# Entry 0's opening in a Fourier-mixing and SoLU kernel: x as stationary operand of the first transform step, its result kept on chip, and the loads and adds around it in another order

## The chip, the cores and the metric

The kernel runs on one core of a Trainium2 chip. The metric is the device time of one execution in microseconds, as the median of several runs. A profile of one execution gives the start and duration of the instructions on each engine: TensorE (PE for matmuls, PEld for loads of the stationary operand), VectorE (DVE), ScalarE (ACT), GpSimd (POOL) and SyncE (SP, which only issues DMAs). ACT and POOL issue DMAs as well.

## The reference

Eight entries of 3136 tokens by 256 channels go through a global filter (a real Fourier transform along the tokens, a product with a complex filter, the inverse transform). All 25,088 tokens then go through a feed-forward block: a product with `w_in`, the SoLU (h times its softmax) with layer normalization, and a product with `w_out`.

```python
def _attn_ref(x, filt_r, filt_i):                 # x: 8 x 3136 x 256
    X = np.fft.rfft(x, axis=1)
    Y = X * (filt_r + 1j * filt_i)[None, :, :]    # 1569 x 256
    return np.fft.irfft(Y, n=x.shape[1], axis=1).astype(np.float32)

def _moe_ref(x, w_in, w_out, g_ln):               # 256 -> 1024 -> 256
    h = x @ w_in
    e = np.exp(h - np.max(h, axis=-1, keepdims=True))
    solu = h * (e / (np.sum(e, axis=-1, keepdims=True) + 1e-09))
    mu = np.mean(solu, axis=-1, keepdims=True)
    var = np.mean((solu - mu) ** 2, axis=-1, keepdims=True)
    return (((solu - mu) / np.sqrt(var + 1e-06) * g_ln) @ w_out).astype(np.float32)
```

`x` and the filters are 4-byte floats; `w_in`, `w_out` and `g_ln` arrive as 8-byte floats.

## The kernel before

**Tiling of the transform.** The 3136 tokens of an entry are seen as 49 (n1) by 64 (n2). A first step transforms over n1 and leaves 25 residues s (`NS`), each with 128 rows (real and imaginary parts of the sums and differences of mirrored n2) and 256 channels. A second step transforms over those rows, residue by residue, with tables `de`. Seven units follow one another, each of four residues but for the last, which has one. A unit is `forward` (matmuls `pb`), `multiply` by the filter (two products on DVE and one add for each of two parts), `inverse` (matmuls `pc`), two ACT copies to `g`, and a store to the DRAM scratch `d2`. The last step (`back`, matmuls `py`) reads `d2` in the other order (the tile `t4`) and fills `y`, the tokens of the feed-forward block.

**The opening** (lines 402 to 604) does this for entry 0 alone, before the main loop, in the order written out by hand. Each engine executes its own instructions, and each queue issues its DMAs, in that order:

1. Lines 512 to 524: loads of x of entry 0 (SP for one half of n2, POOL for the mirrored half, in eight pieces), of the first two pieces of weights (`begin`) and of `de` and filters for the first eight pairs of residues.
2. Lines 525 to 530: the first step, piece by piece. The stationary operand is the 98 x 100 table `wf`, x is the moving one (512 columns), an ACT copy evacuates, and the result goes to the DRAM scratch `d1`.
3. Line 541: `idle_row`, matmuls whose result nobody reads. Lines 547 and 548: `convert` of two pieces of weights from 8 to 4 bytes. Each takes a row of DVE operations, one ACT multiplication (L442) and two POOL operations (L443, L447) for the `w_in` pieces; for the `w_out` pieces L445 on DVE stands in place of L442 and L443.
4. Lines 557 to 564: unit 0's rows are scattered within the chip by 16 DMAs (SP and ACT in turn), and the rows of units 1 to 6 are read back from `d1` by SP, with nine loads of tables for the last residues among them.
5. Lines 565 to 582: the units. `start(i + 2)` comes before unit i's `multiply`, so PE runs ahead by two units. The add of the first part is on DVE, that of the second on POOL; an `idle` matmul stands before each `inverse`. POOL issues four small loads after unit 0 and one `begin` in later units.
6. Lines 583 to 604: 14 `idler` matmuls; SP reads `d2` back in eight pieces, each as 96 rows and 4 rows (L181, L182); `fetch_second` loads six pieces of x of entry 1 (L462); four stores put the filters into `f_dram`; the other weights are converted, `weight_sums` is formed on DVE, and PE runs `back`, 128 rows of the profile in all.

Only units 0 to 5 write what the 96-row reads need; the 4-row reads need unit 6.

**The main loop** (`step`, from line 948) has 196 + 9 steps. A step issues products with `w_in` (L723), the SoLU, products with `w_out` (L844), and jobs of the transforms of entries 1 to 7 at steps fixed by `PLAN`. Its first products need `y` of entry 0 and `w_in`; its first transform jobs need the pieces from `fetch_second`.

One form of matmul of the loop matters for the text: `back_halves` (L372) multiplies 50 x 64 stationary blocks with 49 moving columns in the four quarters of the array, 32 matmuls a call. The profile counts each matmul of this kernel as two records.

Of the kernel before, what the change touches and what calls it, by code (L numbers as in the profile page):

```python
# [49 lines left out]
def dft_tables():  # L50
# [39 lines left out]
    return wf.reshape(NR, NK).astype(f32), wq.reshape(P, 2, 64).astype(f32), \  # L90
# [4 lines left out]
def kernel(  # L95
# [11 lines left out]
    wf_host, wq_host, wi_host, wb_host, de_host = dft_tables()  # L107
# [76 lines left out]
    class Spectrum:  # L184
# [5 lines left out]
        def __init__(self, e, pools, load, load_de):  # L190
            self.e, self.pools = e, pools
            self.load, self.load_de = load, load_de
            self.spare = {}
            self.units = [(i, min(2, NP - i)) for i in range(0, NP, 2)]
            self.xs, self.t1s, self.t2s, self.fs, self.prods, self.gs, self.des, self.spectra, self.diffs = (
                {} for _ in range(9))
# [115 lines left out]

        def multiply(self, i, part, add=nc.vector.tensor_tensor):
# [15 lines left out]
        def inverse(self, i, pss):  # L329
            de, prods = self.des.pop(i), self.prods.pop(i)  # L330
            for r in range(2):
                for u in range(self.shape(i)[0]):
                    rows = slice(NQ * u, NQ * u + NQ)
                    self.product(i, pss[u][NQ * r:NQ * r + NQ], lambda v: de[rows, v, 1, r, :],
                                 prods[r][rows])
# [11 lines left out]
    def fetch_first_back(ch):  # L347
        by_16((nc.sync.dma_start, nc.sync.dma_start), t4s[0, ch],
              d2[0].rearrange("s (a n) c -> (s a) n c", a=4)[:, NCH * ch:NCH * ch + NCH, :])
# [52 lines left out]
    with ExitStack() as st:  # L402
        fpool = pool("fp", 1, stack=st)
        pools = {name: pool(name + "0", bufs, stack=st)
                 for name, bufs in (("r", 1), ("t2", 1), ("p", 2), ("g", 2))}
# [3 lines left out]
        def load_words(src, n):  # L409
            raw = wpool.tile([P, 512, 2], I32, name=f"raw_{n}", tag="raw")  # L410
            nc.gpsimd.dma_start(
# [48 lines left out]
        def fetch_second():  # L460
            for i in range(6):
                second.fetch_x(i, [lambda out, in_: nc.sync.dma_start(out=out, in_=in_)] * 2,  # L462
                               spare_piece(i))

        def load_tables(i0, n, dma):
            de = fpool.tile([P, n, 2, 2, NQ], FP32, name=f"de_{i0}", tag=f"de{i0}")
            dma(out=de, in_=de_dram[i0:i0 + n].rearrange("i p k u q -> p i (k u q)"))
            f = fpool.tile([P, n, 2, C], FP32, name=f"f_{i0}", tag=f"f{i0}")
# [26 lines left out]
        def begin(j):  # L495
            raws[j] = load_words(weights[j][1], j)

# [4 lines left out]
        rows_x = pools["r"].tile([P, NH, C], FP32, name="x_0", tag="r")  # L502

        def fetch_x(h, n0, n, r0, rows, dma):

            first, step = (n0, C) if h == 0 else (N2 - 1 - n0, -C)
            dma(out=rows_x[N1 * h + r0:N1 * h + r0 + rows, n0:n0 + n],
                in_=bass.AP(tensor=x.tensor, offset=x[0].offset + r0 * N2 * C + first * C,
                            ap=[[N2 * C, rows], [step, n], [1, C]]))

        st.enter_context(tc.manual_schedule())
        nc.sync.dma_start(out=wf_t, in_=wf_dram)
        pieces = NH // NCH

        fetch_x(0, 0, NCH, 0, N1 - 1, nc.sync.dma_start)
        fetch_x(0, 0, NH, N1 - 1, 1, nc.sync.dma_start)
        for i in range(pieces):
            if i:
                fetch_x(0, NCH * i, NCH, 0, N1 - 1, nc.sync.dma_start)
            fetch_x(1, NCH * i, NCH, 0, N1, nc.gpsimd.dma_start)  # L520
            if i in (4, 7):
                begin(i // 7)
        load_tables(0, 4, nc.gpsimd.dma_start)
        load_tables(4, 4, nc.gpsimd.dma_start)
        for i in range(pieces):
            sp.xs[i] = rows_x[:, NCH * i:NCH * i + NCH]

            sp.first(i, (0, 1), ps_h.tile([P, 2, 512], FP32, name=f"pa_0_{i}", tag="h"),
                     nc.scalar.copy, sp.xs[i][0:NK])
            sp.store_first(i, 0, lambda out, in_: by_16((nc.scalar.dma_start, nc.sync.dma_start), out, in_))  # L530
# [10 lines left out]
        idle_row(8, "idle")  # L541
# [5 lines left out]
        for j in range(2):  # L547
            convert(j)

        def start(i):  # L550
            sp.fetch_filter(i)
            sp.fetch_de(i)
            sp.forward(i, halves(f"pb_0_{i}"))
# [3 lines left out]
        sp.t2s[0] = t2_0 = pools["t2"].tile([P, 4, C], FP32, name="t2_0_0", tag="t2")  # L557
        for n in range(16):
            (nc.sync, nc.scalar)[n % 2].dma_start(
                out=t2_0[NH * (n % 4):NH * (n % 4) + NH, n // 4, :], in_=rows_x[n:n + 1])  # L560
        for i in range(1, units):
            sp.fetch(i, nc.sync.dma_start, spare_piece(i - 1))
            if i == 2:
                load_tables(8, NP - 8, nc.sync.dma_start)
        for i in range(2):
            start(i)
        for i in range(units):
            if i + 2 < units:
                start(i + 2)
            sp.multiply(i, 0, nc.vector.tensor_tensor)  # L570
            sp.multiply(i, 1, nc.gpsimd.tensor_tensor)
            pss = [ps_t.tile([P, 2, C], FP32, name=f"pc_0_{i}_{u}", tag="t") for u in range(2)]
            idle(pss[0])
# [7 lines left out]
            elif i != 2:  # L581
                begin({1: 2, 3: 3, 4: 4, 5: 5, 6: 6}[i])
# [4 lines left out]
        for ch in range(pieces):  # L587
            fetch_first_back(ch)
        fetch_second()
# [5 lines left out]
        convert(2)  # L595
        begin(7)
        convert(3)
        convert(4)
        weight_sums(w_in_sb)
        for j in (5, 6, 7):  # L600
# [490 lines left out]
```

## Time and profile before

| | |
|---|---|
| median of 3 runs | 1635.9 us (1630.59 to 1640.13) |
| the profiled execution | 1630.59 us, its span 1628.8 us |
| granted TensorE clock of that execution, mean | 0.986 |
| busy over the span | PE 1551.8 us, DVE 1299.9, POOL 1170.6, ACT 903.6 |
| first matmul of the opening | at 8.94 us |
| unit 0's first matmul | at 45.58 us |
| unit 6's store issued | at 81.03 us |
| first product of the main loop | at 106.06 us |

The page gives each engine's busy time, and then the span in 40 slices of 40.7 us. The opening fills the first two and a half. Times of single instructions come from the timeline (start, duration, engine, line, operation, operands, count, and in brackets the idle time before and what ended it). The table of windows gives, for a stretch, each engine's busy time with its number of records, the mean granted clock (PEclk, 1.00 is full), the busy share of the DMA engines, and GB/s.

### The profile page before, as it was taken

What the parts mean: (1) busy time and instruction counts of PE and PEld (TensorE: products, weight loads), DVE (VectorE), ACT (ScalarE), POOL (GpSimd) and SP (SyncE); (2) the same over time, 40 slices, a digit from 0 to 9 for tenths busy, and PEclk for the clock granted to TensorE, in tenths of its full rate; (3) what the DMA queues carried; (4) which work ended last, traced back from release to release, by engine and by line L of the source; (5) the groups of instructions that cost most, each with busy time, mean ns of one, the idle gap of its engine ahead of it and who ended that gap; (6) DMA issues with size and microseconds to landing.
All of it is one profiled execution on the core that took longest, in us unless ns stands there. A gap on an engine that the chain in (4) does not pass through costs nothing. (4 is left out here: it accounts for less than half of the span.)

```text
span 1628.8 us, 36999 instructions
## 1 busy us (share of the span) xinstructions
PE 1551.8 (95%) x12710; PEld 1048.4 (64%) x12710; DVE 1299.9 (80%) x2630; ACT 903.6 (55%) x1772; POOL 1170.6 (72%) x1333
## 2 busy tenths in 40 slices
PE   5798789999999999999999999999999999999997
PEld 1353356666765676666666676666676777777776
DVE  1686777898897989987899779888888777777772
ACT  2134455566565556566556656566555665565662
POOL 4445887678776877797578866888576766677775
PEclk8999999999999999999999999999999999999999
DMA  9888868877788778875787668866875554444443
GB/s 265 245 268 250 231 187 231 230 204 198 206 239 219 198 194 230 240 202 149 222 232 226 186 177 225 239 175 165 222 227 152 130 131 127 104 111 103 110 110 101
DMA packets 377245, 312.13 MB, mean 192 GB/s; under 512 B 62762, under 2 KB 342835, under 8 KB 377059
## 3 DMA queue, kind: packets, MB, share of 16 engines
q1 hardware_dynamic: 304340, 168.63, 40.4%
q0 software_dynamic: 34624, 101.68, 20.8%
q10 hardware_dynamic: 38096, 39.46, 8.0%
q8 instruction: 103, 1.69, 0.5%
q14 instruction: 82, 0.67, 0.1%
HBM read 124.86 MB, written 81.50 MB: 127 GB/s over the span
## 5 line engine op out<-in xcount | busy, mean ns | idle before, releaser
L844 PEld LDWEIGHTS o<-w_out_sb,solu_t 128*128 128x128 f32 x3136 | 383.2, 193 | 51.2 <-issue 43.6
L844 PE MATMUL o<-w_out_sb,solu_t 128*128 128x128 f32 x3136 | 402.2, 276 | 4.1 <-DVE ot L860 3.3
L723 PE MATMUL m<-w_in_sb,s 128*128 128x512 f32 x784 | 397.9, 609 | 8.4 <-ACT h L733 4.7
L844 PEld LDWEIGHTS o<-w_out_sb,u 128*128 128x128 f32 x2352 | 308.0, 192 | 144.4 <-issue 106.2
L844 PE MATMUL o<-w_out_sb,u 128*128 128x128 f32 x2352 | 311.8, 276 | 7.4 <-ACT ot L856 4.7
L723 PE MATMUL m<-w_in_sb,y 128*128 128x512 f32 x588 | 310.0, 610 | 9.2 <-DVE nmax L747 7.1
L771 DVE SCALAR_TENSOR_TENSOR h<-e,rsum,h 128x1024 f32<-128x1024 f32 x196 | 302.7, 1544 | 6.9
L733 ACT COPY h<-m 128x512 f32<-128x512 f32 x294 | 173.2, 589 | 236.7 <-PE m L723 203.4
L702 POOL TENSOR_TENSOR u<-solu_t 128x512 f32<-128x512 f32 x98 | 139.2, 1420 | 227.4 <-DMA solu_t<-turn 133.4
L856 ACT ACTIVATE ot<-o,rs_t 128x128 f32<-128x128 f32 x392 | 143.8, 367 | 259.5 <-PE o L844 241.5
L779 ACT ACTIVATE h<-h,nmu 128x1024 f32<-128x1024 f32 x196 | 225.0, 1148 | 53.4 <-DVE turn L787 53.0
L747 DVE CUSTOM_DVE_ANT_0 h<-m,h 128x512 f32<-128x512 f32 x196 | 133.8, 682 | 145.2 <-ACT h L733 102.0
L787 DVE STREAM_TRANSPOSE turn<-h 128x1024 f32<-128x1024 f32 x196 | 243.1, 1240 | 3.3
L755 ACT ACTIVATE e<-h,nmax 128x1024 f32<-128x1024 f32 x196 | 225.1, 1148 | 10.4 <-DVE h L771 9.9
L702 POOL TENSOR_TENSOR u<-solu_t,u 128x512 f32<-128x512 f32 x98 | 152.6, 1557 | 91.5 <-PE o L844 87.5
L723 PEld LDWEIGHTS m<-w_in_sb,s 128*128 128x128 f32 x784 | 129.2, 192 | 97.2 <-issue 84.6
L723 PEld LDWEIGHTS m<-w_in_sb,y 128*128 128x128 f32 x588 | 95.8, 191 | 108.7 <-issue 49.0
L702 POOL TENSOR_TENSOR u<-u,solu_t 128x512 f32<-128x512 f32 x98 | 164.1, 1674 | 0.9
L860 DVE SCALAR_TENSOR_TENSOR ot<-o,rs_t,ot 128x128 f32<-128x128 f32 x294 | 101.9, 346 | 75.8 <-ACT ot L856 58.4
L702 POOL TENSOR_TENSOR solu_t<-solu_t,solu_t 128x512 f32<-128x512 f32 x98 | 147.5, 1506 | 7.7
L702 POOL TENSOR_TENSOR s<-y 128x128 f32<-128x128 f32 x196 | 97.0, 495 | 0.4
L372 PEld LDWEIGHTS py<-wb_t,t 50*64 50x64 f32 x3584 | 57.8, 134 | 44.3 <-issue 20.9
(116 smaller groups left out, 1961.7 us busy)
## 6 DMA issues: line engine op xcount, KB each, us to landing
solu_t<-turn SPq DMA_DIRECT2D x784, 128.0 KB
out_dram<-ot SPq DMA_DIRECT2D x196, 128.0 KB
t<-d POOLq DMA_DIRECT2D x112, 200.0 KB, 6.2
d<-x POOLq DMA_DIRECT2D x100, 200.0 KB, 5.3
f<-f_dram POOLq DMA_DIRECT2D x39, 512.0 KB, 7.0
d<-g POOLq DMA_DIRECT2D x39, 512.0 KB, 4.9
t<-d ACTq DMA_DIRECT2D x37, 512.0 KB
x<-in_x_dram SPq DMA_DIRECT2D x112, 98.0 KB
```

The lines of the kernel that those rows point to most:

```text
L372: nc.tensor.matmul(out=views[g][64 * h:64 * h + 64, cb, i, :], lhsT=t4[rows, i, c0:c0 + 64], rhs=wb_t[rows, 0:N1], start=True, stop=True)
L702: nc.gpsimd.tensor_tensor(out=out, in0=in0, in1=in1, op=op)
L723: nc.tensor.matmul(out=ms[j, bank], lhsT=lhsT, rhs=w_in_sb[:, w, :], start=m in (1, 2, 7), stop=True, skip_group_check=True)
L733: nc.scalar.copy(out=h_half(k, i), in_=ms[j, 0])
L747: nc.vector.tensor_tensor_reduce(out=h_half(k, i), in0=ms[j, bank], in1=h_half(*kept), scale=1.0, scalar=sofar, op0=ALU.add, op1=ALU.min, ...
L755: nc.scalar.activation(out=e, in_=hs[k], func=AFT.Exp, bias=nmaxs.pop(k)[:, 1:2], scale=-1.0, accum_out=esum)
L771: nc.vector.scalar_tensor_tensor(out=solu, in0=e, scalar=rsum, in1=solu, op0=ALU.mult, op1=ALU.mult, accum_out=nmu)
L779: nc.scalar.activation(out=solu, in_=solu, func=AFT.Square, bias=nmu, scale=-float(DFF), accum_out=variances[g][:, i:i + 1])
L787: nc.vector.transpose(out=turns[g][:, :, i, :], in_=solus[k].rearrange("p (f j) -> p f j", j=32))
L844: nc.tensor.matmul(out=pos[p, bank], lhsT=lhs[:, f, :], rhs=w[:, f, :], start=f == 0 and m in (1, 2, 7), stop=True, skip_group_check=True)
L856: nc.scalar.activation(out=out_half(p, *to)[0], in_=pos[p, 0], func=AFT.Copy, scale=rs)
L860: nc.vector.scalar_tensor_tensor(out=ot, in0=pos[p, bank], scalar=rs, in1=out_half(p, *kept)[0], op0=ALU.mult, op1=ALU.add)
```

## The change

**x by channel.** x of entry 0 lies on chip in two blocks of 64 partitions (128 channels each, n1 on the partitions), so a DMA run is 512 bytes in place of 1 KB. SP loads one block and ACT the other, in four quarters of n2. Before them DVE and POOL clear partitions 32 to 63, in four pieces. DVE (POOL for two of eight) forms sums and differences of mirrored n2 in `y`, which is still free.

**First step with x as stationary operand.** For each of 128 channels there are four matmuls: a 49 x 64 block of x is stationary, and 25 columns of a small table `wx` move. Seven groups of up to 20 channels are evacuated by one ACT copy each, straight into the rows that the second step reads. `d1` of entry 0, its stores and read-backs, the scatter and the `idle` row are gone. Eight `warm` matmuls go before the groups, one `keep` matmul follows each.

**Units.** `forward_whole` multiplies with all 128 rows at once and 64 stationary columns, in place of 64 x 64 blocks. It has its own tables `de0`, half as large again. Both adds are on POOL. The `idle` before `inverse` is gone.

**Order.** All tables and filters go through SP behind x. Weights 0 to 3 are begun by POOL ahead of the units; three `convert`s stand before the units and the fourth behind them. Behind the units SP reads all eight 96-row pieces of `d2` first and the eight 4-row pieces after them, then loads weights 4 and 5, three pieces of entry 1, weights 6 and 7, and three more pieces; the stores of the filters follow.

```diff
+        def forward_whole(self, i, pss):
+            de, i0 = self.des[i], self.units[i][0]
+            for v in range(self.units[i][1]):
+                for r in range(2):
+                    for u in range(self.shape(i)[0]):
+                        nc.tensor.matmul(out=pss[r][NQ * u:NQ * u + NQ, v, :], lhsT=de[:, v, r, u, :],
+                                         rhs=self.turned[:, 2 * (i0 + v) + u, :], start=True, stop=True)
+            self.spectra[i] = pss
...
-    def fetch_first_back(ch):
-        by_16((nc.sync.dma_start, nc.sync.dma_start), t4s[0, ch],
-              d2[0].rearrange("s (a n) c -> (s a) n c", a=4)[:, NCH * ch:NCH * ch + NCH, :])
+    def fetch_first_back(ch, part):
+        rows = (slice(0, 96), slice(96, NK))[part]
+        nc.sync.dma_start(out=t4s[0, ch][rows], in_=d2[0].rearrange("s (a n) c -> (s a) n c", a=4)[
+            rows, NCH * ch:NCH * ch + NCH, :])
...
+        nc.sync.dma_start(out=wx_t, in_=wx_dram)
+        pieces = NH // NCH
+        quarter = NH // 4
+        for i in range(4):
+            (nc.vector, nc.gpsimd)[i % 2].memset(x_q[32:64, :, quarter * i:quarter * i + quarter, :], 0.0)
+        for i in range(4):
+            for h in range(2):
+                fetch_x(0, h, quarter * i, quarter, 0, N1 - 1, nc.sync.dma_start)
+                fetch_x(1, h, quarter * i, quarter, 0, N1 - 1, nc.scalar.dma_start)
+            if i == 0:
+                for h in range(2):
+                    fetch_x(0, h, 0, NH, N1 - 1, 1, nc.sync.dma_start)
+                    fetch_x(1, h, 0, NH, N1 - 1, 1, nc.scalar.dma_start)
         nc.sync.dma_start(out=wf_t, in_=wf_dram)
-        for i in range(pieces):
-            sp.xs[i] = rows_x[:, NCH * i:NCH * i + NCH]
-
-            sp.first(i, (0, 1), ps_h.tile([P, 2, 512], FP32, name=f"pa_0_{i}", tag="h"),
-                     nc.scalar.copy, sp.xs[i][0:NK])
-            sp.store_first(i, 0, lambda out, in_: by_16((nc.scalar.dma_start, nc.sync.dma_start), out, in_))
...
+        for i0, n in ((0, 4), (4, 4), (8, NP - 8)):
+            load_tables(i0, n, nc.sync.dma_start)
...
+        for i in range(4):
+            mirror(i, 0, nc.vector)
+            mirror(i, 1, nc.gpsimd if i % 2 else nc.vector)
+            if i == 1:
+                begin(0)
+            if i == 3:
+                for n in range(8):
+                    nc.tensor.matmul(out=ps_t.tile([P, 512], FP32, name=f"warm_{n}", tag="t"),
+                                     lhsT=sums_x[both, :, 0, 16], rhs=sums_x[both, 0:64, 0, 16:24],
+                                     start=True, stop=True)
+                for j in (1, 2, 3):
+                    begin(j)
+
+        for c0 in range(0, P, 20):
+            n = min(20, P - c0)
+            ps = ps_h.tile([P, 2, 512], FP32, name=f"pa_0_{c0}", tag="h")
+            for k in range(n):
+                for g in range(2):
+                    for part in range(2):
+                        rows = slice(64 * g, 64 * g + N1)
+                        nc.tensor.matmul(
+                            out=ps[64 * part:64 * part + 64, g, NS * k:NS * k + NS],
+                            lhsT=sums_x[rows, c0 + k, :, :].rearrange("p j m -> p (j m)"),
+                            rhs=wx_t[rows, part, 0:NS], start=True, stop=True)
+            nc.scalar.copy(
+                out=rows_x[:, 0:NS, :].rearrange("p s (g c) -> p g s c", g=2)[:, :, :, c0:c0 + n],
+                in_=ps[:, :, 0:NS * n].rearrange("p g (k s) -> p g s k", s=NS))
+            nc.tensor.matmul(out=ps_t.tile([P, 512], FP32, name=f"keep_{c0}", tag="t"),
+                             lhsT=sums_x[both, :, 0, 16], rhs=sums_x[both, 0:64, 0, 16:24],
+                             start=True, stop=True)
...
-        idle_row(8, "idle")
...
-        for j in range(2):
+        for j in range(3):
             convert(j)
...
-            sp.forward(i, halves(f"pb_0_{i}"))
+            sp.forward_whole(i, halves(f"pb_0_{i}"))
...
-        sp.t2s[0] = t2_0 = pools["t2"].tile([P, 4, C], FP32, name="t2_0_0", tag="t2")
-        for n in range(16):
-            (nc.sync, nc.scalar)[n % 2].dma_start(
-                out=t2_0[NH * (n % 4):NH * (n % 4) + NH, n // 4, :], in_=rows_x[n:n + 1])
-        for i in range(1, units):
-            sp.fetch(i, nc.sync.dma_start, spare_piece(i - 1))
-            if i == 2:
-                load_tables(8, NP - 8, nc.sync.dma_start)
...
-            sp.multiply(i, 0, nc.vector.tensor_tensor)
+            sp.multiply(i, 0, nc.gpsimd.tensor_tensor)
             sp.multiply(i, 1, nc.gpsimd.tensor_tensor)
...
-            idle(pss[0])
...
-            elif i != 2:
-                begin({1: 2, 3: 3, 4: 4, 5: 5, 6: 6}[i])
+        convert(3)
         idle_row(14, "idler")
...
-        for ch in range(pieces):
-            fetch_first_back(ch)
-        fetch_second()
+        for part in range(2):
+            for ch in range(pieces):
+                fetch_first_back(ch, part)
+        for j in (4, 5):
+            begin(j, nc.sync.dma_start)
+        fetch_second(0, 3)
+        for j in (6, 7):
+            begin(j, nc.sync.dma_start)
+        fetch_second(3, 6)
...
-        convert(2)
-        begin(7)
-        convert(3)
-        convert(4)
         weight_sums(w_in_sb)
-        for j in (5, 6, 7):
+        for j in (4, 5, 6, 7):
             convert(j)
```

## The prediction

> **What bounds the kernel now.** I read the windows first, to see where the time is not the main loop's.
>
> ```profile
> 45.60:81.00 35.40, 26.32 (x218) 12.70 (x218) 25.52 (x42) 6.82 (x13) 14.14 (x16) 0.90 0.91 268
> 81.00:91.50 10.50, 10.50 (x26) 4.57 (x25) 10.19 (x15) 1.34 (x2) 6.13 (x5) 1.00 0.74 243
> 91.50:106.00 14.50, 14.50 (x130) 14.38 (x129) 14.15 (x24) 7.30 (x15) 3.08 (x2) 1.00 0.81 226
> ...
> 200.00:1570.00 1370.00, 1350.12 (x11611) 934.63 (x11604) 1152.60 (x2352) 812.05 (x1608) 1025.16 (x1162) 1.00 0.69 187
> ```
>
> After 200 us PE works 98.5% of the time, and nothing there is changed. The change can only move the point at which the loop begins, at 106 us. The timeline gives the chain up to it.
>
> ```profile
> 28.78 1.22 ACT L442 ACTIVATE raw<-raw 128x512 f32<-128x512 int32 x2 [0.76 <-DMA f<-in_filt_r_dram]
> ...
> 35.49 10.16 PE L534 MATMUL idle<-f,de 128*128 128x512 f32 x16 [8.86 <-DMA f<-in_filt_i_dram]
> ...
> 39.84 1.32 POOL L443 TENSOR_TENSOR raw<-raw,power 128x512 f32<-128x512 f32 x1
> ...
> 45.58 0.68 PEld L301 LDWEIGHTS pb<-t,de 64*64 64x64 f32 x14 [0.76 <-PE idle L534]
> ...
> 52.73 1.27 POOL L324 TENSOR_TENSOR pi<-pi,pt 128x512 f32<-128x512 f32 x1 [7.61 <-DVE pt L323]
> ...
> 78.51 0.37 ACTq L343 DMA_DIRECT2D d<-g  x1
> ...
> 81.03 0.34 ACTq L343 DMA_DIRECT2D d<-g  x1
> ...
> 86.48 0.33 SPq L181 DMA_DIRECT2D t<-d  x1
> 87.10 0.27 SPq L182 DMA_DIRECT2D t<-d  x1
> ...
> 91.80 8.40 PE L395 MATMUL py<-wi_t,t 100*128 100x98 f32 x74
> ...
> 106.06 1.93 PE L723 MATMUL m<-w_in_sb,y 128*128 128x512 f32 x4
> ```
>
> Units from 45.58, stores of units 5 and 6 at 78.51 and 81.03, read-back from 86.48, the last step from 91.5 to 106.06. That step is 128 records without a gap. One of its eight pieces takes PE 1.8 us, while SP's later issues of `t<-d` (91.29, 93.19, 94.62, 96.03), each of which waits for an earlier piece, are 1.4 to 1.9 us apart: once the first piece is there, the transfer hides behind PE. The clock is lost in gaps: the `idle` matmuls behind 9 us of waiting run at a granted 0.53 (window 30 to 40), and the first weight loads of the program are 0.85 us apart for 4.4 us, and 0.43 later.
>
> **The change part by part**, in time from the span's start.
>
> *x.* SP's first big load waits for the clearing of its partitions. DVE's memset takes 0.17 us for 128 elements and 0.06 for 4, so 1.9 us for 2048, until 2.8. x is 3.2 MB. The first 20 us moved 199 GB/s with the DMA engines 89% busy: 16.1 us, so x is there at 18.9. Shorter runs may cost 3 us more; the 230 GB/s of window 10 to 20 would save 2.
>
> *Sums and warm-up.* The last sums are ready some 2.5 us later (POOL: two 512-element rows of 1.27), at 21.4. PE cannot begin before all of x is there: one stationary block spans every n2. The eight `warm` matmuls start with three quarters of x, at 14.9 + 1.4 = 16.3. They are 16 records, 5 at 0.85 and 11 at 0.44: 9.1 us, until 25.4. They, not x, set the start.
>
> *First step.* 128 x 4 matmuls are 1024 records with 25 columns. The nearest row is L372: 64 records of 50 x 64 by 49 columns start at 392.93, and the next product at 394.01, 16.9 ns a record. Were the columns the cost, it would be 8.6 ns. I take 16.9, since the stationary block is as wide: 17.3 us (8.8 to 25). Each of seven `keep` matmuls costs two records of 0.44: 6.2. The evacuations (1.01 us for 1024 columns) lie beside PE but for the last. Unit 0 starts at 25.4 + 17.3 + 6.2 + 1.0 = 49.9, against 45.58: the removed stores, scatter, `idle` row and read-back were shorter than what replaces them.
>
> [...]
>
> *Units.* Both adds are now on POOL, and so is what is queued ahead. ACT's multiplications for the three `convert`s come after all seven evacuations in ACT's order (before, L442 stood at 28.78 behind the eighth copy, with DVE's part of the first weights done at 23.6). POOL's four operations for two weights took 39.84 to 45.12, 2.64 a weight. So unit 0's first add waits: 49.9 + 0.67 + 7.9 = 58.5. What is queued behind it: 12 adds of 1.27 for units 0 to 5 (15.2) and four loads after unit 0 (53.94 to 56.57, 2.65): 76.4. From POOL's add at 54.0 to the store's issue at 56.27 it was 2.3: unit 5's store at 78.7, where it was 78.51. Unit 6 (two adds of 0.77) follows at 80. DVE's five operations a unit become four of 0.6 and are no bound. PE needs 16 records of 256 columns (0.21 us each) for `forward_whole`: 1.7 us if the two column halves work side by side, as quarters do in L372, 3.4 if not; no row has this form. With the inverse's 0.9 the first hides behind POOL's 2.6 a unit. The removed `idle` (1.1) was off the chain. The two `g` buffers allow one unit in 3.0 us (68.35, 71.36, 74.25), up to 2 us more in all.
>
> *Read-back.* POOL-issued 512 KB stores land in a median 4.9 us; unit 5's took until 86.48, 8.0, beside 512 KB weight loads that are gone here. I take 5: reads from 83.7. Now all 96-row pieces go ahead of the 4-row pieces. Piece 0 cannot be used until its four rows are in, behind all eight others on the same queue. Before, the first piece came 4.8 us after its issue and the others 1.45 apart: 15 us for all, less 1.7 for the weights that shared the engines: 97.0 against 91.5. The order wins a unit at the front and loses the overlap. If the four rows overtook, `back` would start at 88.5.
>
> [...] No row here shows a small transfer behind eight large ones.
>
> *Last step.* The 14 `idler` matmuls (28 records, 12.3 us) end near 91.5, so 5.5 us of idle precede `back`. As after the 9 us gap, 5 records at double length: 2.1. End: 97.0 + 2.1 + 14.4 = 113.5, 7.4 us later than 106.06.
>
> *Given back.* SP's pieces of entry 1 follow the read-back, not `back`: PE's 1.33 us wait for them at 112.2 goes. At 142.93 PE waited 2.97 us for DVE, which waited for x of entry 2, queued on SP behind the filters' stores; that queue moves by some 5 to 6 us, the loop by 7, so I take half, 1.5 (0 to 3). Weights 4 to 7 now reach DVE after the read-back; `convert` ended at 112.76, 6.7 us behind the loop's start, and will end near 118, 4.5 behind. If that bound the loop, the shift would be 5 to 6.
>
> Sum: 7.4 - 1.3 - 1.5 = +4.6 us on the profiled execution's 1630.59, which is 5.3 below the median (its span is 1628.8, 1.8 lies outside). On the median 1635.9 + 4.6 = 1640.5.
>
> **The rivals.** About 0.5%, 8.2 us, is what a measurement of this kernel can tell from no change.
>
> A, the forecast: the opening ends as late as before, within 8.2 us either way. 0.42.
>
> B, slower: `forward_whole`'s column halves do not overlap. PE then needs 4.3 us a unit where POOL needs 2.6, five times 1.7 more: +13, 1649. It decides as soon as a unit takes PE over 3.3 us (five times 0.7 added to 4.6). [...] For it: no row with 128 rows and 64 columns. Against: L372's quarters overlap in both directions. 0.32.
>
> C, faster: short matmuls cost by their columns (-8.5), and the 4-row pieces do not wait for the large ones (-8.5, and no cold start, -2.1): 4.6 - 19.1 = -14, 1622. It needs 12.8 us off my sum, so neither half alone suffices. For it: 16.9 ns may be the columns' cost, since 49 columns at 0.84 ns (0.43 us for 512) fill 41 of a quarter's 68 ns. Against: the 64-wide stationary block is unchanged. 0.26.
>
> The range reaches to C's price below, and above to B's with 6 us for slow x and a cold clock in the first step: 1622 to 1655.
>
> **What would show it.** Right: unit 0's first `pb` near 50, its first POOL add near 58 behind three conversions, `py` from 97 after an idle PE, first `m` near 113. [...] The forecast falls if the first `m` comes before 100 or after 118.

## The result, and the profile after

The changed kernel takes 1686.2 us (median of 4 runs, 1683.6 to 1687.4) where the kernel before takes 1633.2 (4 runs, 1628.8 to 1640.1): a ratio of 1.032, 95% interval 1.028 to 1.036. The profiled spans are 1681.8 and 1628.8, 53.0 us apart; the forecast was 4.6, less than the 8.2 that the prediction itself takes for no change. So neither the loss nor its size was foreseen.

The timeline of PE, from the first step to the loop's third product (columns: start, duration, engine, line, operation, records, and in brackets the idle time before with what ended it; start and duration in us from the span's start):

```profile
20.21 8.85 PE L575 MATMUL warm<-y 113*128 113x512 f32 x16 [20.21 <-DVE y L564]
28.99 2.53 PE L588 MATMUL pa<-wx_t,y 49*64 49x25 f32 x160
31.45 1.24 PE L595 MATMUL keep<-y 113*128 113x512 f32 x2
32.62 0.88 PE L588 MATMUL pa<-wx_t,y 49*64 49x25 f32 x45
36.37 2.62 PE L588 MATMUL pa<-wx_t,y 49*64 49x25 f32 x115 [2.87 <-issue]
...
46.85 0.84 PE L588 MATMUL pa<-wx_t,y 49*64 49x25 f32 x21 [1.89 <-issue]
47.62 2.08 PE L595 MATMUL keep<-y 113*128 113x512 f32 x2
49.63 4.48 PE L588 MATMUL pa<-wx_t,y 49*64 49x25 f32 x160
...
120.69 27.60 PE L416 MATMUL py<-wi_t,t 100*128 100x98 f32 x128 [5.19 <-DMA t<-d]
148.07 2.86 PE L781 MATMUL m<-w_in_sb,y 128*128 128x512 f32 x4
...
165.84 3.78 PE L781 MATMUL m<-w_in_sb,s 128*128 128x512 f32 x4 [11.41 <-POOL s L760]
```

Three things were not in the forecast. The first step runs near the forecast pitch for one group (160 records in 2.53, 15.8 ns each, forecast 16.9), stops twice while it waits for nothing that the profile shows ("issue"), and afterwards takes 4.48 for the same 160. The last step takes 27.60 for 128 records in place of 14.4. And the third product waits 11.41 for the pair sums, where before it came 7.7 behind the first (106.06 and 113.78). The windows of the same stretches (busy time and records of PE, PEld, DVE, ACT and POOL, then the granted clock, the DMA share and GB/s) show why both steps are long: the clock.

```profile
33.00:33.50 0.50, 0.50 (x33) 0.39 (x25) 0.47 (x2) 0.50 (x1) 0.00 (x0) 1.00 1.05 396
33.50:36.40 2.90, 0.03 (x4) 0.03 (x4) 0.81 (x2) 0.41 (x1) 0.00 (x0) 1.00 1.10 301
37.00:37.50 0.50, 0.50 (x44) 0.50 (x40) 0.00 (x0) 0.00 (x0) 0.00 (x0) 0.85 1.14 240
47.00:60.00 13.00, 13.00 (x333) 9.95 (x337) 0.00 (x0) 1.98 (x2) 0.00 (x0) 0.50 0.03 8
...
120.69:148.07 27.38, 27.38 (x128) 27.38 (x129) 2.65 (x6) 7.29 (x15) 0.00 (x0) 0.50 0.78 260
200.00:1620.00 1420.00, 1388.07 (x11855) 951.51 (x11855) 1199.47 (x2426) 837.56 (x1653) 1071.21 (x1211) 1.00 0.69 189
```

The clock goes to 0.50 between 37.0 and 37.5, nearly 4 us after the first stop began and 1 us after work had resumed, and stays there although PE is busy 100% of the time. From 200 us on PE works 97.8% of the time at 1.00: all is decided in the opening, as forecast.

Stage by stage, with the forecast's terms (a first read is the first `t<-d` issue):

| | forecast | measured | miss |
|---|---|---|---|
| first step begins | 25.4 | 28.99 | +3.6 |
| first step, to unit 0's `pb` (72.75) | 24.5 | 43.8 | +19.3 |
| unit 0 to unit 5's store (103.01) | 28.8 | 30.3 | +1.5 |
| store to first read (105.93) | 5.0 | 2.9 | -2.1 |
| first read to `py` (120.69) | 13.3 | 14.8 | +1.5 |
| last step, to the first `m` (148.07) | 16.5 | 27.4 | +10.9 |
| from the first `m` on, against before | -2.8 | +11.0 | +13.8 |

The misses add up to 48.4 = 53.0 - 4.6. Three rows carry them, and the experiments take one each. Most runs are single executions, and those of the kernel before, taken beside them, lie between 1625.0 and 1645.2; so the verdicts rest on positions in the trace, and where a run was repeated its interval is given. "After" below is the changed kernel, 1686.2.

### The profile page after: what moved, and what is told of

Same layout as the page of the kernel before. It is cut to its first block, busy times and chain, and to the rows that moved or that the text cites. A ratio compares the mean times of both kernels' runs of the same rounds, so it can differ in the third digit from the quotient of the medians.

```text
span 1681.8 us, 38933 instructions
## 1 busy us (share of the span) xinstructions
PE 1584.2 (94%) x13702; PEld 1088.0 (65%) x13702; DVE 1317.0 (78%) x2631; ACT 901.8 (54%) x1771; POOL 1169.0 (70%) x1314
## 4 chain that ended last, share of the span: by engine, by line
PE 66%; DMA 13%; DVE 8%; issue 6%; POOL 3%; SPq 2%; ACT 1%; ACTq 0%; DVEq 0%; POOLq 0%
PE o L902 28%; PE m L781 27%; DMA solu_t<-turn 4%; PE py L393 3%; DMA x<-in_x_dram 3%; PE pc L312 2%; PE pa L280 2%; DMA out_dram<-ot 2%; PE py L416 2%; PE pb L312 2%; DVE turn L845 1%; DMA rs_t<-rows 1%; DVE h L829 1%; DMA t<-d 1%; SPq L857 1%
## 5 line engine op out<-in xcount | busy, mean ns | idle before, releaser
L781 PE MATMUL m<-w_in_sb,s 128*128 128x512 f32 x784 | 397.0, 607 | 21.4 <-POOL s L760 11.4
L902 PEld LDWEIGHTS o<-w_out_sb,solu_t 128*128 128x128 f32 x3136 | 383.4, 193 | 49.6 <-issue 43.6
L902 PE MATMUL o<-w_out_sb,u 128*128 128x128 f32 x2352 | 313.0, 276 | 10.7 <-ACT ot L914 6.6
L829 DVE SCALAR_TENSOR_TENSOR h<-e,rsum,h 128x1024 f32<-128x1024 f32 x196 | 298.6, 1523 | 6.9
L760 POOL TENSOR_TENSOR u<-solu_t 128x512 f32<-128x512 f32 x98 | 135.5, 1382 | 225.4 <-DMA solu_t<-turn 158.2
L805 DVE CUSTOM_DVE_ANT_0 h<-m,h 128x512 f32<-128x512 f32 x196 | 133.8, 682 | 160.6 <-ACT h L791 115.7
L760 POOL TENSOR_TENSOR solu_t<-solu_t,solu_t 128x512 f32<-128x512 f32 x98 | 153.9, 1570 | 7.7
L760 POOL TENSOR_TENSOR s<-y 128x128 f32<-128x128 f32 x196 | 101.5, 518 | 0.4
```

The costliest lines, as they stand in the source:

```text
L760: nc.gpsimd.tensor_tensor(out=out, in0=in0, in1=in1, op=op)
L781: nc.tensor.matmul(out=ms[j, bank], lhsT=lhsT, rhs=w_in_sb[:, w, :], start=m in (1, 2, 7), stop=True, skip_group_check=True)
L805: nc.vector.tensor_tensor_reduce(out=h_half(k, i), in0=ms[j, bank], in1=h_half(*kept), scale=1.0, scalar=sofar, op0=ALU.add, op1=ALU.min, ...
L829: nc.vector.scalar_tensor_tensor(out=solu, in0=e, scalar=rsum, in1=solu, op0=ALU.mult, op1=ALU.mult, accum_out=nmu)
L902: nc.tensor.matmul(out=pos[p, bank], lhsT=lhs[:, f, :], rhs=w[:, f, :], start=f == 0 and m in (1, 2, 7), stop=True, skip_group_check=True)
```

## Experiments: the last step

**e_idler.** Theory: the gap of 5 us ahead of `py` costs the clock, and nothing else is slow there.

```
-        idle_row(14, "idler")
+        idle_row(24, "idler")
```

> The changed kernel with 24 idler matmuls in place of 14, so that TensorE has work (8.8 us more) until past the arrival of the rows of the last step. Theory 1 (the clock): the last step ran 27.6 us at a granted 0.50 because TensorE stood idle for 5.2 us before it, and 98 moving columns do not bring the clock back; now it runs at 1.00 and takes 14.4 us, the first product of the loop comes at about 139 in place of 148 (the idlers end at 124.3, 3.6 us after the rows arrive), the run 9 to 13 us faster. Rival (the last step is slow for another reason, such as ScalarE's copies or the transfers): it still takes 27 us and the first product comes 3 us later.

1677.2. PE's timeline:

```profile
102.40 20.87 PE L601 MATMUL idler<-f,de 128*128 128x512 f32 x48
123.11 14.43 PE L416 MATMUL py<-wi_t,t 100*128 100x98 f32 x128
137.37 1.91 PE L781 MATMUL m<-w_in_sb,y 128*128 128x512 f32 x4
```

Twenty wide records (ten matmuls) more, no gap, and the same 128 records take 14.43: 2.4 us later to start, 10.7 earlier to end. The time follows by 9.

**e_back.** The other way to close the gap: each 96-row piece is followed by its own 4-row piece, as before.

```
-        for part in range(2):
-            for ch in range(pieces):
+        for ch in range(pieces):
+            for part in range(2):
```

> The changed kernel with the read-back in the order of the kernel before: each 96-row piece is followed by its 4 rows. Theory 1 (the 4-row pieces wait behind all the large ones on the queue): the first piece is complete some 5 us after the first issue (about 111), so the last step starts right behind the idlers at 115.5, without a gap, at full clock, and ends at about 130: first product at 130 in place of 148, the run 18 us faster. Rival (the order costs nothing, small pieces overtake): the last step still starts at 120.7 and still runs at half clock; no change.

1672.7.

```profile
114.28 14.43 PE L416 MATMUL py<-wi_t,t 100*128 100x98 f32 x128
```

`py` starts right behind the idlers and takes 14.43; the first `m` is at 128.55 in place of 148.07. Only 13.5 of these 19.5 us reach the end, since the third product still waits 12.08 for the pair sums.

**b_part.** The same part alone, in the kernel before: all 96-row pieces first.

> The kernel before with one part of the change alone: all eight 96-row pieces of the read-back ahead of the eight 4-row pieces. Theory 1 (a small piece waits behind the large ones on its queue): the last step starts at 98 to 101 in place of 91.5, TensorE idles 6 to 9 us behind the idlers, its clock falls to 0.50, and the last step takes 27.6 us in place of 14.4: first product at 126 to 129 in place of 106, and the time 15 to 23 us above the kernel before. Rival (the step of the forecast that only the start moves, and the clock is back after 4 us): first product at 115, 8 to 9 us above. Third possibility: the small pieces overtake, no change.

1650.1, against 1635.6 for the kernel before, one execution each.

```profile
100.08 27.60 PE L396 MATMUL py<-wi_t,t 100*128 100x98 f32 x128 [10.18 <-DMA t<-d]
127.47 3.41 PE L725 MATMUL m<-w_in_sb,y 128*128 128x512 f32 x4
```

Its first `t<-d` is issued at 84.04, so `py` can use its first piece 16 us after it, behind all the others; the first `m` is 21.4 us late (106.06 before), of which 14.4 are left at the end, a little less than expected. One reordering of 16 transfers costs about 0.9%.

## Experiments: the first step

The stops come at fixed places. Counting PE's records from `warm` on, the changed kernel stops after 223 and 479. In all 13 kernels here that have this step, every stop over 0.3 us that nothing but "issue" ended (19 of them, in 11 kernels) comes after record 223, 351 or 479, which are multiples of 128 apart. A record is a matmul and its weight load, so 128 are 256 instructions; an instruction queue (q8) moves 111 packets of 16 KB in the whole execution. PE's 13,702 records and as many weight loads would fill 107 of them at 256 instructions a packet. And the packets keep time with the stops: in the changed kernel one begins at 33.70 and one at 44.08, and PE resumes 2.7 and 2.8 us later (36.37 and 46.85). I read this as PE having run out of instructions; what a packet holds no row shows. The queues' view of the changed kernel around the first stop, 33 to 37 us (packets, MB, share of the 16 DMA engines' span):

```profile
q1 hardware_dynamic: 1079, 1.20, 108.0%
q8 instruction: 1, 0.02, 1.5%
```

One packet among 1079 of SP's tables. Theory: a packet comes late because the tables hold the engines; the stop loses the clock; thin matmuls do not win it back. The rival: thin matmuls lose the clock by themselves.

**e_hold.** Tables from the fifth pair on and weights 2 and 3 wait for the evacuation of the sixth group (through a store that reads it), and `convert(2)` follows the units.

```
-        for i0, n in ((0, 4), (4, 4), (8, NP - 8)):
-            load_tables(i0, n, nc.sync.dma_start)
+        load_tables(0, 4, nc.sync.dma_start)
...
-                for j in (1, 2, 3):
-                    begin(j)
+                begin(1)
...
+            if c0 == 100:
+                nc.sync.dma_start(out=d1[0][0:1, 0, c0:c0 + 16], in_=rows_x[0:1, 0, c0:c0 + 16])
+                load_tables(4, 4, nc.sync.dma_start)
+                load_tables(8, NP - 8, nc.sync.dma_start)
+                for j in (2, 3):
+                    begin(j, nc.sync.dma_start)
...
-        for j in range(3):
+        for j in range(2):
             convert(j)
...
+        convert(2)
         convert(3)
```

> The changed kernel with the transfers out of the first step's way: behind x only the tables of the first four pairs and the first two weights are loaded; the other tables and the third and fourth weights are issued by SP after the evacuation of the sixth group (a 64-byte store that reads its result holds the queue), and the third conversion moves behind the units. Theory 1 (TensorE's instructions are late behind the loads; the 2.9 us gap in the second group costs the clock): no gap over 1 us, the granted clock stays 1.00, the groups are 3.7 us apart, and the first step takes 25 to 27 us in place of 42: unit 0 at about 55. Rival (thin matmuls cannot hold the clock, gap or no gap): the clock falls to 0.50 in the second or third group all the same, and unit 0 comes at about 72. Either way units 2 and 4 will wait for their tables (4.0 MB at 225 GB/s from the sixth group on: 18 us), so the gain at the loop's start is smaller than that at unit 0.

1676.1.

```profile
33.98 2.53 PE L586 MATMUL pa<-wx_t,y 49*64 49x25 f32 x160
...
37.60 2.40 PE L586 MATMUL pa<-wx_t,y 49*64 49x25 f32 x139
41.67 0.54 PE L586 MATMUL pa<-wx_t,y 49*64 49x25 f32 x21 [1.67 <-issue]
```

Half held: the stop after 223 is gone, the one after 479 remains with the DMA engines idle, and at 43.6, 3.6 us after it began, the clock falls; unit 0 starts at 66.19, between the theory's 55 and the rival's 72. The tables are not the whole cause. Without them the packets still come 3.5 us apart (32, 35, 39, 42, 46 us), and this step uses up 128 records in 2.9 us, its `keep` included.

**e_hold8.** The same with a slower first step: groups of 16 channels, a wide matmul (a pair of records) after every 8, so that 128 records last 4.3 us. The late loads now wait for the evacuation of the seventh group.

```
-        for c0 in range(0, P, 20):
-            n = min(20, P - c0)
+        for c0 in range(0, P, 16):
+            n = 16
...
+                if k == 7:
+                    nc.tensor.matmul(out=ps_t.tile([P, 512], FP32, name=f"keep_{c0}_mid", tag="t"),
+                                     lhsT=sums_x[both, :, 0, 16], rhs=sums_x[both, 0:64, 0, 16:24],
+                                     start=True, stop=True)
```

> The previous kernel with the tables held back (the tables of the last pairs and two weights issued after most of the first step), and a wide keep matmul after every 8 channels in place of 20, so that 128 records of the first step take TensorE 4.3 us in place of 2.9. [...] Theory 1 (the supply of instructions, one packet per 128 records): 4.3 us a packet is slower than the supply, so no gap over 0.5 us is left, the granted clock stays at 1.00 through the first step, and its 16 half-groups take 34 to 36 us: unit 0 at about 66, as in the kernel with only the tables held back, in spite of nine more keeps. Rival (thin matmuls lose the clock by themselves, or the gap has nothing to do with the number of instructions): the clock falls to 0.50 within 15 us of the start, the half-groups take 4.3 us each, unit 0 comes after 85.

1679.3. No stop, and the windows of the whole first step show a clock of 1.00:

```profile
30.20:45.00 14.80, 14.80 (x462) 10.79 (x462) 3.27 (x7) 3.76 (x4) 0.00 (x0) 1.00 0.02 3
45.00:65.80 20.80, 20.80 (x597) 14.23 (x596) 0.00 (x0) 4.33 (x6) 0.00 (x0) 1.00 0.15 45
```

Unit 0 starts at 65.80, 7 us earlier than in the changed kernel, with 18 more wide records in the step. Thin matmuls with a wide pair after every 8 channels kept a clock of 1.00 here. (With a pair after every 20, e_hold kept it at 1.00 from 30.4 until after its stop; a step without any wide pairs was not run.) The units then wait for the late tables: POOL's adds stand idle for 5.91 us ahead of 89.90, and the time is no better than e_hold's.

**e_keep8.** The slower step of e_hold8 alone, the tables loaded as in the changed kernel.

> Changed kernel with one edit: groups of 16 channels and a wide matmul pair after every 8 channels of the first step; tables and weights are loaded as in the changed kernel. Theory (the instruction packets of 128 records come every 3 to 4 us and are held up by the table loads; thin matmuls at 15.8 ns use them up in 2.9 us with the keep, half-groups of 2.22 us for 64 records use them up in 4.4): the first stall, after some 223 records, is gone, since these are used up only at 36.7; the second, after some 479 records, is under 1.5 us; the granted clock is 1.00 for over 80% of the first step, unit 0 starts at 65.5 to 68.5 (changed kernel 72.75, with held-back tables 65.8), and the time is 1677 to 1681. Rival: the table loads delay the packets as before, a gap of over 1.5 us near 34 or 45 remains, and with it a clock of 0.5 for the rest: unit 0 at 73 or later, time 1686 or more.

1696.1: the rival of this run held. The first stop is gone, the second is there, and what follows is the same instructions as in e_hold8 at half the clock.

```profile
29.70:45.90 16.20, 16.20 (x464) 11.39 (x463) 4.11 (x9) 3.76 (x4) 0.00 (x0) 1.00 1.06 298
45.90:47.70 1.80, 0.01 (x1) 0.00 (x0) 0.00 (x0) 0.00 (x0) 0.00 (x0) 1.00 0.15 40
49.00:50.00 1.00, 1.00 (x2) 0.30 (x2) 0.00 (x0) 0.72 (x1) 0.00 (x0) 0.64 0.00 0
60.00:81.00 21.00, 21.00 (x340) 12.13 (x336) 0.00 (x0) 3.08 (x5) 0.00 (x0) 0.50 0.01 2
```

With the two kernels side by side, the load order decides: tables on the engines until 45.9 (share 1.06) and a stop of 1.80, or none (0.02) and no stop. One stop of 1.80 us costs 15.7 us here (unit 0 at 81.45 against 65.80). I had expected the slower pace to be enough by itself; it is not. Nor do the wide pairs, 2.08 of every 3.9 us, bring the clock back.

**e_keep3.** Three wide pairs a group in place of one, nothing else.

```
+            for n_keep in range(3):
...
```

> The changed kernel with three keep matmuls after each group in place of one. Theory 1 (a gap takes the clock, thin matmuls hold it but do not bring it back, several us of wide ones do): the clock falls to 0.50 after the first gap as before, is at 1.00 again after the next keeps or the ones after them (three at half clock are 5.2 us of wide work), and falls again at the next gap; later groups, with no loads left beside them, run at 1.00 in 2.5 + 3.0 us each, and unit 0 comes at 68 to 74, no later than now (72.75), in spite of 14 more matmuls. Rival (the clock follows the share of wide work): the groups settle at one clock between 0.5 and 1 from the start, and unit 0 comes after 80.

1686.0. Stops of 0.63 and 1.89 remain, but the clock returns after each:

```profile
36.00:39.00 3.00, 3.00 (x81) 1.96 (x75) 0.00 (x0) 0.99 (x1) 0.00 (x0) 0.71 1.00 256
39.00:42.00 3.00, 3.00 (x33) 1.35 (x31) 0.00 (x0) 0.00 (x0) 0.00 (x0) 0.72 1.08 293
42.00:45.00 3.00, 1.76 (x119) 1.66 (x111) 0.00 (x0) 0.00 (x0) 0.00 (x0) 1.00 0.99 208
48.00:51.00 3.00, 3.00 (x20) 0.98 (x21) 0.00 (x0) 0.00 (x0) 0.00 (x0) 0.52 0.00 0
51.00:54.00 3.00, 3.00 (x158) 2.87 (x155) 0.00 (x0) 0.64 (x1) 0.00 (x0) 1.00 0.02 5
```

Unit 0 starts at 72.82: the clock won pays for the extra records and no more. Three wide pairs in a row restored the clock, one pair at a time did not. A stop of as little as 0.18 (63.77 to 63.95, after record 991) was also followed by a stretch at 0.50, from 64.6 to 68.0.

## Experiments: the loop's start

**e_order.** In the program as built, VectorE's finish of the loop's first step (L805) stands in the middle of `convert(4)`. It needs the first product, which is now late, and the conversions stand behind it:

```profile
127.69 0.42 DVE L457 TENSOR_SCALAR w_out_sb<-raw 128x512 int32<-128x512 int32 x1
151.08 0.69 DVE L805 CUSTOM_DVE_ANT_0 h<-m,h 128x512 f32<-128x512 f32 x1 [22.97 <-ACT h L791]
```

POOL's additions and, behind them, its pair sums wait for these conversions. The edit issues step 0 behind the last conversion (`convert` returns its last instruction for it).

```
-            convert(j)
+            last_convert = convert(j)
...
-        for k in range(blocks + LAG):
+        with tc.issue_after(last_convert.ins):
+            step(0)
+        for k in range(1, blocks + LAG):
```

> The changed kernel with one thing different: VectorE issues the main loop's first step only after the last weight conversion of the opening. In the changed kernel the loop's first row maximum stands in the middle of the fifth conversion and holds VectorE from 128 to 151 us. Theory 1 (VectorE's order): conversions 5 to 8 are done before the last step of the transform ends, GpSimd's sums are early, and the 11.4 us wait of TensorE before its third product (154.4 to 165.8 us) goes: the first step of the loop is about 11 us shorter, the run some 11 us below the changed kernel's 1686, with the first product still at 148. Rival (the wait is for something else, such as the filters' stores or the pieces of entry 1): the wait stays within 2 us of 11.4 and the time is unchanged.

1676.2: the third product comes at 157.90 with no wait, the first at 150.10.

**e_back_order.** Both together should give both gains.

> The changed kernel with two parts undone: the read-back in the order of the kernel before, and VectorE's first loop operation behind all weight conversions. Alone they gave 13.5 and 10 us; alone the read-back's order had left a wait of 12.1 us for GpSimd's sums. Theory 1 (two separate losses, the second hidden behind the first where the loop starts early): first product at 128 to 129, third product no later than 142 (the last weights land after the read-back and are converted beside the last step), and a time of 1658 to 1664. Rival (the loop's start is set by the arrival of the last weights and the pieces of entry 1, whatever the order): the third product stays at 150, and the time at 1672.

1672.5, as with e_back alone: the rival's time, but not its reason, and the third product comes at 157.11, not 150.

```profile
156.08 0.45 POOL L760 TENSOR_TENSOR s<-y 128x128 f32<-128x128 f32 x1 [11.51 <-DMA x<-in_x_dram]
```

The conversions end at 148.9, but POOL's first pair sum waits 11.51 us. The profile names the semaphore that came last, of a load of x. In the program as built the pair sum also waits for the four stores to f_dram, on SP behind the weights that the change moved there (issued at 139 to 147). It shares no data with them. It shares memory: its tile `s14` lies at byte 142848, where `de_8` lies in the changed kernel, since the wider tables pushed up what follows them in the opening's memory; before, entry 0's row tile lay there, and the wait was for the `t<-d` reads. The tables' pool is free only when its last readers, the stores, are done. In the changed kernel itself this wait hid behind VectorE's. The next two experiments test this.

**e_pool.** On top of e_back_order, the two loop pools in the other order.

```
-    upool = pool("up", 2)
     hpool = pool("hp", 2)
+    upool = pool("up", 2)
```

> Changed kernel with 96-row and 4-row pieces in turn, the loop's step 0 issued behind the last conversion, and the two loop pools upool and hpool allocated in the other order, so that the pair sums no longer lie on memory of the opening's tables (de_8). Without the last of the three edits: 1672.5, third product at 157.1 behind a wait of 11.9 us for the pair sums, which ended when the four f_dram stores landed. Theory: the pair sums wait only because their memory belonged to the tables' pool, which is free when the f_dram stores (issued 139 to 147) have landed; now they run right behind GpSimd's last addition (144.6), the third product comes at 145 to 147, no wait of over 3 us is left in front of it, and the time is 1661 to 1665. Rival: the sums, or the product, wait for something else that ends as late (the x pieces of entry 1, or h behind VectorE's conversions, which end at 148.8): third product at 152 or later, time 1667 to 1673.

1674.3, no gain: now `h` lay on that memory. The pair sums ran at 132.02, and ACT shows where the wait went, with its cause by name:

```profile
157.53 0.59 ACT L791 COPY h<-m 128x512 f32<-128x512 f32 x1 [25.59 <-DMA f_dram<-f]
```

**e_s14.** On top of e_back_order, `s14` in a pool of its own behind `hpool`; the stores' memory then falls to a tile that is used later.

```
     hpool = pool("hp", 2)
+    s14pool = pool("s14p", 2)
...
-        s14 = upool.tile(
+        s14 = s14pool.tile(
```

> Changed kernel with the pieces in turn, step 0 behind the last conversion, and the pair sums' tile s14 in a pool of its own behind hpool, so that neither it nor h lies on memory of the opening's tables. (With the two pools swapped whole, h came to lie there and took over the wait: 25.6 us for f_dram, first L805 at 158.2, time 1674.3.) Theory: the wait belongs to that memory and to nothing else. Then no instruction of the loop's first step waits for f_dram; the pair sums run within 4 us of the last py copy, ACT copies h right behind the first products, the first L805 comes behind VectorE's conversions at 148 to 149.5, and the time is 1661 to 1666. Rival: the x pieces of entry 1 or the conversions hold the loop as long, so that the time stays at 1670 to 1675 although the wait is gone.

1661.3 (4 runs, 1651.6 to 1663.7), ratio 1.017, interval 1.011 to 1.022.

```profile
130.52 0.47 POOL L761 TENSOR_TENSOR s<-y 128x128 f32<-128x128 f32 x1 [20.91 <-ACT y L419]
147.16 0.68 DVE L806 CUSTOM_DVE_ANT_0 h<-m,h 128x512 f32<-128x512 f32 x1
```

The sums run behind the last `py` copies, the finish behind the conversions, and the time is where the theory put it. The cause was memory: `s14` moved to other memory, and its wait went; with `h` there (e_pool), `h` waited.

## Experiments: the parts together

**e_all.** e_pool and e_keep8 in one.

> Changed kernel with the four edits together: pieces in turn, step 0 behind the last conversion, pools in the other order, wide matmuls after every 8 channels. Theory: the gains lie on one chain and add up, about -13.5 (pieces in turn), -10 to -11.5 (order and pools), -6 (first step): 1655 to 1660, ratio 1.013 to 1.016 against the kernel before; what remains is the later start and the longer first step (unit 0 at 66 to 68 against 45.6). Rival: an earlier first step is eaten by the tables (loaded at about 63) and by the units' own queue on GpSimd, and the time stays that of the three edits, 1661 to 1667.

1687.7, ratio 1.032 (1.027 to 1.038): neither theory. It combined two edits of which each had failed, for reasons found only afterwards: two stops (1.18 and 0.51), unit 0 at 88.31 at half the clock, and the wait on `h`.

**e_all2.** e_s14 and e_hold8 in one.

> The same, and the first step as in the run without a gap (tables from the fifth pair on and two weights held back until an evacuation, a wide matmul pair after every 8 channels). Theory: the first step runs at a clock of 1.00 throughout, unit 0 starts at 65 to 67, the units wait for the late tables as in that run, and its gain of about 7 us adds to the others: 1654 to 1660, ratio 1.013 to 1.017 against the kernel before; what is left is unit 0 at 66 in place of 45.6. Rival: what the first step gains is lost where the loop waits for VectorE's conversions and entry 1's pieces: time within 2 us of the run without it.

1658.3 (4 runs, 1655.5 to 1663.4), ratio 1.015, interval 1.010 to 1.021. No stop, clock 1.00 from 28.8 to 64.3, unit 0 at 64.34, first `m` at 126.64. The loop's row L736 (`ps_mean`) starts at 158.21; it is 165.10 in e_s14, 184.38 in the changed kernel, 129.61 before. Of those 6.9 us against e_s14 the medians show 2.9, within the spread of the runs, so how much of this gain reaches the end stays open. Of the changed kernel's 53 us about 28 are explained by causes that could be removed one by one, the last 2.9 within the spread. Of what is left, about 23 to 25 us, 18.8 stand at unit 0 (64.34 against 45.58); the rest was not taken apart. No version here beats the kernel before.

## Why the prediction was wrong

*The first step* is the largest failure. The term of 1024 records at 16.9 ns, 17.3 us, plus 6.2 for `keep`, was right as a pitch: 15.8 ns measured, 3.6 us a group. It failed in taking the pitch for the duration. Before, PE never ran 1024 short records in a row, so no row showed whether that pitch lasts. Here 128 records last 2.9 us, and the packets come every 3.5 (e_hold) and, beside the tables, 4.2 and 6.2 apart (33.70, 37.85 and 44.08 in the changed kernel). The range had "a cold clock in the first step" within 6 us; with the stops, 4.8 us, it made the step 19.3 longer, since it lasted to the end of the step. By the term, copies would be 3.6 us apart (160 records at 16.9 ns and a `keep` of 0.88); they came 6.4 apart (54.17 to 60.59). The 25 us at the upper end of the term no run shows; at 15.8 ns the 1024 records make 16.2.

*The last step* was mis-sized: "5 records at double length: 2.1" measured 13.2 (27.60 against 14.43). I took the recovery from the `idle` row of before, which is 512 columns wide. With 98 columns the clock did not return in 27 us of unbroken work (0.50 from 120.69 to 148.07). Wide rows brought it back in e_keep3 (0.71 and 0.72 in the two windows from 36 to 42 us, 1.00 in the next); the 98-column rows, and the 25-column rows with one `keep` a group, busy 100% of the time, did not. The gap itself was right: forecast 5.5, measured 5.19, for the reason given (each piece's four rows behind the eight large transfers); e_back and b_part confirm it.

*The loop's start.* "Given back" had the loop lose less than the shift, and the conversions no bound ("4.5 behind"). That took VectorE's order to be the text's, conversions first; the built order had the finish among them, and the conversions ended near 169.6, 21.5 behind the first `m`. From the first `m` on the loop lost 11.0 where the sum gave 2.8 back. With VectorE's order and the read-back mended, the memory under `s14` still cost a wait of 11.9 ahead of the third product (e_back_order). None of this was in a rival.

*Right or nearly:* the three conversions ahead of unit 0's first add on POOL (9.4 us behind unit 0's `pb`, forecast 8.6; VectorE's third conversion waited for POOL to free `power`); the pace of POOL's adds (1.27 each); the overlap of `forward_whole`'s column halves (16 records in 1.95, forecast 1.7, so rival B's mechanism is refuted). Rival C's two halves failed as well: columns alone would make 8.6 ns a record, where 15.8 were measured, and the last step began 14.8 us behind the first read. The read-back came 2.9 us behind the store, forecast 5.0. *Off, and left open:* the first step began 3.6 us late. `warm` waited until 20.21, forecast 16.3, for a sum of DVE (18.27 to 20.15). x was late: the first sum could start only at 10.93, and from 10 to 20 us the DMA engines moved 162 GB/s where the prediction took 199. The sums were slow too: the two of DVE that began while one of POOL's ran took 4.01 each, the other four 1.88 to 1.90. No run took the two apart.

## What to carry to other kernels

In these runs a long row of very short matmuls stopped for 0.5 to 3.3 us at a time, 128 records or a multiple apart, which I read as instructions arriving late: 3.5 us between packets without loads beside them, up to 6.2 with the tables there. So look for idle time that only "issue" ends, at record counts a fixed multiple apart, and keep large transfers off that stretch. Ahead of thin matmuls, close any gap of PE with wide ones until the moment they start, since a clock lost there was not won back by them here (0.50 from 47.0 to 72.5 in the changed kernel). When a stage's tiles change size, look again at what the next stage's tiles lie on, and whether an order written for early data still holds when the data are late.

## What the runs showed of the hardware

- In these kernels PE's stops of over 0.3 us that only "issue" ended come after record 223, 351 or 479, 128 records apart or a multiple of it. In the changed kernel PE resumes 2.7 and 2.8 us after a 16 KB packet of the instruction queue begins; without the tables beside them (e_hold) five packets came 3.5 us apart on average (from 32 to 46).
- Every such stop of 0.63 us or more that began at a clock of 1.00 was followed by 0.50 (changed kernel, e_hold, e_keep3, e_keep8, e_all) or by `keep` pairs of 2.08 us in place of 1.23 or 1.24 (e_order, e_idler, e_back, e_back_order, e_pool, e_s14). The fall came at 37.4 for a stop from 33.50 (changed kernel) and at 43.6 for one from 40.0 (e_hold), 3.9 and 3.6 us from its start; PE had been busy again for 1 to 2 us by then. The two first steps without a stop (e_hold8, e_all2) stayed at 1.00.
- At 0.50, 27.60 us of 98-column matmuls without a gap do not restore it, nor do 31 us in which half the time is 512-column pairs, one pair at a time (e_keep8); three such pairs in a row do (e_keep3). What the clock follows, no run here shows.
- 49x64 blocks in four quarters of the array with 25 columns take 15.8 ns a record at a clock of 1.00 (160 in 2.53 us) and 28 at 0.50 (160 in 4.48).
